# A linear-attention kernel with a dense gated layer: second group's attention later, key rows copied by GpSimd, three f-tiles begun on two thirds of their tokens, last outputs on two queues

## The chip, the cores and the metric

The kernel runs on one core of one Trainium2 chip. Its engines are TensorE (PE, with its weight loads shown apart as PEld), VectorE (DVE), ScalarE (ACT), GpSimd (POOL) and SyncE (SP), whose queue issues most of the DMAs. The metric is the device time of one execution in microseconds (us).

## The reference

A linear attention with a decaying state runs over 4 batches, 8 heads, 768 steps and a head size of 48. Its result, as 3072 tokens of 384 values, goes through a dense layer of 2048 columns with the gate h·tanh(softplus(h)).

```python
for t in range(S):                      # per batch and head
    cur = (u * k[t]) v[t]^T
    y[t] = r[t] (state + cur)
    state = w * state + k[t] v[t]^T
x = y as (B * S, H * D)                 # 3072 x 384
h = x @ w_in                            # 384 x 2048
g = h * tanh(softplus(h))
out = g @ w_out                         # 2048 x 384
```

## The kernel before, in words

**Attention.** A step handles a chunk of 64 positions for two of the four batches, so 128 tokens; there are 24 steps, and even and odd steps work on different batches with buffer sets 0 and 1 (`G`, `Wt`, `KI`). Of each step: `load_step` and `load_v` fetch r, k and v; `scale` (L483, DVE) multiplies r and k by powers of the decay; `halves` (L467) copies halves of them to the buffers, by ACT or DVE in the first three steps and by DMA (L471) later; `diag` (L502 on ACT or L504 on DVE) scales keys by u; `keys` (L539) makes the key rows; `attend` lets PE make scores (`pa`, L554) and DVE mask them (L594, the second mask takes the diagonal); `outputs` lets PE make the result (`yt`, L607, L620) and the next state (`st`, L664). ACT evacuates both (L693, L695, L680), PE transposes (L751), and ACT and DVE write the tokens to `x` (L720, L723).

`KI` holds key rows and, in the rows `DROWS`, the decay by which the state is carried: a diagonal block `ident * w^64`, written once for each of the two sets by eight ACT rows (`state_decay`, L263). Those of set 0 are made at the start; those of set 1 by `second_decay`, spread between other rows.

**Dense layer.** Three steps make a group of 384 tokens; there are eight groups. For a group the 16 f-tiles of 128 columns are gone through: `up` (L802 for group 0, which uses float32 weights whole, L778 for the others, in three products of float32r parts) accumulates an f-tile in one of two PSUM buffers `hp`; ACT or DVE copies it to `hb` (L892); four f-tiles make a batch, on which ACT runs three activations with two table loads (L813, L816, L819) and DVE multiplies (L828); `down` (L847, L778) then accumulates three outputs `acc0` to `acc2`. After a group they are copied to `ob` (L859) and written out (L860). The weights come as 64-bit floats: `convert_low` (L340, ACT) and `convert` (L357 or L359, L361, L363, L366, L368) make float32 of them during group 0, and `split` (L383, L385) makes the two parts.

**Order.** Each engine's instructions stand in one fixed order, which a planner in the kernel (`Flow`) makes from estimated costs when the program is built: each piece of work is a thread that yields the events it needs and the engine time it takes, and where two engines could do a copy the planner chooses. In PE's spare time ahead of the first f-tile the planner puts `keep_warm` products on zeros (L283). `place` says after which f-tile of the group before a step's attention may begin: it spreads the three steps of a group over the fractions from `LO0` to `HI0` (group 1) or `LO1` to `HI1` (the others) of that group's 16 f-tiles.

```python
n0, n = BESIDE.get(g) or (LAST[g - 1] + 1 - NF, NF)
lo, hi = (LO0, HI0) if g == 1 else (LO1, HI1)
at = (2 * (s - starts[g]) + piece) / (2 * GROUPS[g])
return n0 + min(n - 1, int((lo + at * (hi - lo)) * n))
```

Of the kernel before, what the change touches and what calls it, by code (L numbers as in the profile page):

```python
# [10 lines left out]
F32 = mybir.dt.float32  # L11
# [5 lines left out]
AF = mybir.ActivationFunctionType  # L17
# [4 lines left out]
B, H, S, D = 4, 8, 768, 48  # L22
NP = H // 2
# [6 lines left out]


SOON = 3
LENT = 2

UDIAG = 6
# [6 lines left out]
KT = DM // 128  # L42
NF = DFF // 128
NT = B * S
# [3 lines left out]
WG = 2  # L48
# [6 lines left out]
DROWS = (slice(0, D), slice(64, 64 + D))  # L55
# [3 lines left out]
GROUPS = [3] * 8  # L59
# [7 lines left out]
RK_BUFS = 2  # L67
GS = 2
LAG_US = 24.9
LO0, HI0, LO1, HI1 = 0.05, 0.9, 0.05, 0.8  # L70
AHEAD, HOLD_W = 2, 8
LAT, LAT0 = 0.15, 0.13
WARM0, WARM_MIN, FILL = 32, 0.3, 0.6
# [9 lines left out]
UNITS = [(ph, g, f) for ph, (g, f0, f1) in enumerate(PHASES) for f in range(f0, f1)]  # L83

BATCH, AT = [], []
for ph, (g, f0, f1) in enumerate(PHASES):
    n = 1 << int(math.log2(COLS // (128 * GROUPS[g])))
# [95 lines left out]
def pe(us):  # L183
    return {"pe": us}
# [3 lines left out]
def rwkv_mish_kernel(ctx, tc, rkT, rkN, vN, wT, w_in, w_out, consts, rkF, vF, wF, uF, outT):  # L188
    nc = tc.nc
# [5 lines left out]
    ps = ctx.enter_context(tc.tile_pool(name="ps", bufs=1, space=PSUM))  # L195
# [11 lines left out]
    ident = cst[:, 128:256]  # L207
# [4 lines left out]
    early = const.tile([128, 1], F32, name="early")  # L212
# [5 lines left out]
    KI = [const.tile([128, 2, 2, NP, D], F32, name=f"KI{i}") for i in range(2)]  # L218
# [24 lines left out]
    w64 = pw[:, 6]  # L243
# [13 lines left out]
            mul = pw[:, m].unsqueeze(1).unsqueeze(3).broadcast_to([128, 2, NP, n])  # L257
            nc.vector.tensor_tensor(out=both(n, C - 2 * n, n), in0=both(0, C - n, n), in1=mul, op=ALU.mult)

    def state_decay(i, par, p):  # L260

        r = DROWS[par]
        nc.scalar.activation(  # L263
            KI[i][r, par, :, p, :], ident[r, r].unsqueeze(1).broadcast_to([D, 2, D]), AF.Copy, scale=w64[r, p : p + 1]
        )

    def token_table():
# [7 lines left out]
                )  # L275
        nc.scalar.copy(out=TKn, in_=t[:, : NP * D].rearrange("t (p d) -> t p d", d=D))

    idle = ps.tile([128, 512], F32, name="idle", tag="hp", bufs=2)

    def keep_warm(n):  # L280

# [5 lines left out]
    nc.vector.tensor_tensor(out=uw, in0=wu[:, 1], in1=wc, op=ALU.mult)  # L287
    for par in range(2):
        for p in range(NP):
            state_decay(0, par, p)  # L290
    token_table()

    flow = Flow(FREE)
    flow.events.update(READY)
    flow.fill = lambda us: keep_warm(int(us * FILL / 0.112))
    ok = const.tile([32, 1], I32, name="ok")

    def second_decay():
        for par in range(2):
            for p in range(NP):  # L300
                yield {"act": 0.3}
                state_decay(1, par, p)
        flow.set("decay")

    def check_range():

# [19 lines left out]
    raws, wholes, parts = {}, {}, {}  # L326
# [65 lines left out]
    xs = {}  # L392
# [237 lines left out]
    def outputs(s):  # L630
        q = s % 2
        last = s >= NS - NQ

        more = TURN <= s < NS - 1
        yield f"moved{s}"
        yield f"placed{s}"
        yield f"keys{s}"
        yield f"v{s}"
        if s == 1:
            yield "decay"  # L640
        if s:
            yield f"y{s - 1}"
            yield f"state{s - 1}"
            if GROUPS[0] <= s <= TURN:
                yield f"x{s - 1}"
        if more:
            yield f"scaled{s + 1}"
            yield f"masked{s}"
        yield from paced(s, 1)
        yield pe((1.0 if last else 1.8 if s >= TURN else 2.0) + (0.9 if more else 0))  # L650
        y = ps.tile([128, 512], F32, name="yt", tag="yt")
        st = ps.tile([128, 512], F32, name="st", tag="st")

        for p in range(NP):
            for a in range(2):
                for b in range(2):
                    tokens(q, y, p, a, b) if s < TURN else rows(q, y, p, b, a)
        if not last:
            for c in range(2):
                for p in range(NP):  # L660
                    for par in range(2):
                        k = slice(0, (128, 112)[par])
                        n = (c * NP + p) * D
                        nc.tensor.matmul(  # L664
                            st[DROWS[par], n : n + D],
                            lhsT=KI[q][k, par, c, p, :],
                            rhs=Wt[q][k, par, c, p, :],
                            start=True,
                            stop=True,
                        )  # L670
        if more:
            pas[s + 1] = scores(s + 1, loaded[s + 1][0][:, 1], "pa")
            flow.set(f"scores{s + 1}")
        flow.set(f"out{s}")
        flow.start((evacuate_y if s < TURN else direct)(s, y), rank(s) - L_FIN)
        if not last:
            for par in range(2):
                r = DROWS[par]
                engine = yield {**act(384), **dve(384)}
                (nc.scalar.copy if engine == "act" else nc.vector.tensor_copy)(  # L680
                    out=Wt[q][r, par].rearrange("d c p e -> d (c p e)"), in_=st[r, : 2 * NP * D]
                )
        flow.set(f"state{s}")
# [108 lines left out]
    def by_tile(o, t):  # L792
        return t[:, : o.n * o.T].rearrange("p (j t) -> p j t", j=o.n)

    def up(o, j):
        f, T = o.f + j, o.T
        hp = ps.tile([128, 512], F32, name="hp", tag="hp", bufs=2)
        w = (wholes if o.whole else parts)[0, f // WG]
        for k in range(KT):
            fs = slice((k * WG + f % WG) * 128, (k * WG + f % WG + 1) * 128)  # L800
            if o.whole:
                nc.tensor.matmul(hp[:, :T], lhsT=w[:, fs], rhs=o.x[:, 0, k, :T], start=k == 0, stop=k == KT - 1)  # L802
                continue
            three(
                hp[:, :T], w[:, 0, fs], w[:, 1, fs], o.x[:, 0, k, :T], o.x[:, 1, k, :T],
                k == 0, k == KT - 1,
            )
        return hp[:, :T]
# [45 lines left out]
    def put(engine, mt, T, cols):  # L854
        if cols.stop == NT and mt == KT - 1:
            ob = work.tile([128, COLS], F32, name="ob", tag="fa", bufs=1)
        else:
            ob = stage.tile([128, TM], F32, name="ob", tag="we", bufs=WE_BUFS)
        (nc.scalar.copy if engine == "act" else nc.vector.tensor_copy)(out=ob[:, :T], in_=accs[mt][:, :T])  # L859
        nc.scalar.dma_start(outT[mt * 128 : (mt + 1) * 128, cols], ob[:, :T])  # L860


    batches = {}
# [1 line left out]
    def up_tile(n):  # L865
        ph, g, f = UNITS[n]
        b, j = AT[n]
        T = GROUPS[g] * 128
        if f == 0:
            for s in range(starts[g], starts[g] + GROUPS[g]):  # L870
                yield f"x{s}"
        if j == 0 and 2 <= b < len(BATCH) - 1:
            yield f"gated{b - 2}"
        yield f"{'w' if g else 'v'}0,{f // WG}"
        if n >= 2:
            yield f"h{n - 2}"
        yield pe(unit_us(n))
        flow.fill = None
        if j == 0:
            batches[b] = new_batch(T, xs[g], f, len(BATCH[b]), not g, b == len(BATCH) - 1)  # L880
        o = batches[b]
        flow.start(evacuate(n, o, j, up(o, j)), n - L_EVAC)
        if n == BATCH[b][-1]:
            flow.start(gate(b, o, BATCH[b]), n - L_GATE)
        if n == LAST[g]:
            flow.set(f"ups{g}")
        if not g and f % WG == WG - 1:
            flow.set(f"used{W_ORDER.index((0, f // WG))}")
# [72 lines left out]
    def ffn():  # L961
        d = 0
        for n in range(len(UNITS) + 1):
            if n < len(UNITS):
                yield from up_tile(n)
                flow.set(f"u{n}")
            while d < len(UNITS) and AFTER[d] <= n:
                yield from down_tile(d)
                d += 1
# [3 lines left out]
            flow.start(thread(s), rank(s) + k / 1000 - (L_V if group[s] and thread is load_v else 0), 0.0)  # L973
    flow.start(check_range(), -100, 0.0)
    flow.start(load_weights(), -500, 0.0)
    flow.start(second_decay(), -1000.5, 0.0)
    for c in range(len(W_ORDER)):
        i, f = W_ORDER[c]
        n = FIRST[f * WG]
        flow.start(convert_low(c), (AFTER[n] - L_OUT if i else n - L_IN) + c / 1000 - AHEAD, 0.0)  # L980
        flow.start(convert(c), (AFTER[n] - L_OUT if i else n - L_IN) + c / 1000, 0.0)
        n += NF
        flow.start(split(c), (AFTER[n] - L_OUT if i else n - L_IN) + c / 1000, 0.0)
    flow.start(ffn(), 1000, 0.0)
    flow.run()
    assert not flow.parked, list(flow.parked)
# [152 lines left out]
```

## Time and profile before

| | |
|---|---|
| time, median of 3 runs | 531.26 us (529.8, 531.26, 535.85) |
| the profiled execution | 530.0 us, span of its trace 528.2 us |
| PE busy | 510.8 us (97% of the span) |
| PE weight loads busy | 470.1 us (89%) |
| ACT busy | 402.8 us (76%) |
| DVE busy | 323.3 us (61%) |
| POOL busy | 6.0 us (1%), 19 instructions |
| PE's mean granted clock | 0.994 |

The profile comes from one execution. Busy shares are means over the whole span, and this kernel has two stages with different loads: the first 50 us, with the attention of group 0 and the conversion of the weights, and the rest, where the dense layer runs. They have to be read apart. PE's busy time in the first stage contains the products on zeros.

### The profile page before, as it was taken

Reading aid. Unit: us, or ns where it says so; the run is one execution under the profiler, and the core shown is the slowest. Engines: PE = TensorE matmul, PEld = TensorE weight load, DVE = VectorE, ACT = ScalarE, POOL = GpSimd, SP = SyncE. Lnnn points to the kernel's source line nnn. Section 1 sums busy time; section 2 is a strip of 40 time slices with the busy share of each in tenths; the row PEclk is TensorE's granted clock in tenths of the full one; section 3 lists DMA queues with packets and bytes.
Section 4 is the critical chain, followed back from the end, with each engine's and each line's share of the span. In section 5 each row is a group of like instructions: output and inputs, shape, how many; then the busy total and the mean of one; then the engine's idle time right before and its main releaser. Section 6 shows DMA issues by size and latency. Waiting matters only on the chain.

```text
span 528.2 us, 11442 instructions
## 1 busy us (share of the span) xinstructions
PE 510.8 (97%) x4765; PEld 470.1 (89%) x4765; DVE 323.3 (61%) x489; ACT 402.8 (76%) x501; POOL 6.0 (1%) x19
## 2 busy tenths in 40 slices
PE   8887999999999999999999999999999999999994
PEld 6754666687999999999999999999999999999993
DVE  6998998765676575474664475474474473334341
ACT  6999957669798668667887768667687767777882
POOL 4000000000000000000000000000000000000000
PEclk9999899999999999999999999999999999999998
DMA  8998444113443244323443243323333250001001
GB/s 238 414 374 274 130 132 130 45 37 92 115 115 106 59 149 114 86 74 103 119 114 104 63 151 108 97 59 107 117 116 104 66 153 17 2 2 45 1 0 49
DMA packets 31051, 57.88 MB, mean 110 GB/s; under 512 B 6064, under 2 KB 19248, under 8 KB 30992
## 3 DMA queue, kind: packets, MB, share of 16 engines
q1 hardware_dynamic: 27392, 52.13, 33.9%
q10 hardware_dynamic: 3600, 4.95, 2.7%
q8 instruction: 39, 0.64, 0.5%
q14 instruction: 20, 0.16, 0.1%
HBM read 36.80 MB, written 4.72 MB: 79 GB/s over the span
## 4 chain that ended last, share of the span: by engine, by line
PE 80%; ACT 7%; DVE 4%; DMA 3%; SPq 2%; issue 2%; ACTq 0%; DVEq 0%
PE hp L778 30%; PE acc L778 27%; PE hp L802 6%; PE acc L847 5%; PE pa L554 5%; PE yt L620 3%; PE st L664 2%; SPq L743 1%; DMA rk<-in_rkT_dram 1%; ACT fa L816 1%; PE yt L607 1%; ACT wraw L340 1%; DMA rkn<-in_rkN_dram 1%; ACT L819 1%; DVE hb L828 1%
## 5 line engine op out<-in xcount | busy, mean ns | idle before, releaser
L778 PE MATMUL hp<-x,w 128*128 128x384 f32 x1008 | 197.0, 338 | 0.5 <-DMA x<-rkn 0.5
L778 PE MATMUL acc<-gh,w 128*128 128x384 f32 x672 | 187.8, 335 | 1.0 <-ACT gh L831 1.0
L778 PEld LDWEIGHTS hp<-x,w 128*128 128x128 f32 x1008 | 175.6, 188 | 3.8 <-DMA x<-rkn 0.8
L778 PEld LDWEIGHTS acc<-gh,w 128*128 128x128 f32 x672 | 122.8, 188 | 1.4 <-ACT gh L831 1.3
L778 PE MATMUL acc<-gl,w 128*128 128x384 f32 x336 | 112.3, 334 | 0.1
L892 ACT COPY hb<-hp 128x384 f32<-128x384 f32 x100 | 47.3, 474 | 59.6 <-PE hp L778 47.0
L828 DVE TENSOR_TENSOR hb<-hb,fa 128x768 f32<-128x768 f32 (+1 forms) x58 | 51.8, 927 | 39.9 <-ACT fa L819 39.9
L892 DVE COPY hb<-hp 128x384 f32<-128x384 f32 x28 | 15.6, 557 | 86.8 <-PE hp L778 84.1
L778 PEld LDWEIGHTS acc<-gl,w 128*128 128x128 f32 x336 | 63.1, 188 | 0.4 <-DVE gl L834 0.4
L831 ACT CAST gh<-hb 128x768 fp32r<-128x768 f32 (+1 forms) x58 | 47.2, 817 | 21.0 <-DVE hb L828 20.8
L834 DVE TENSOR_TENSOR gl<-hb,gh 128x768 fp32r<-128x768 f32 (+1 forms) x58 | 52.7, 928 | 7.6 <-ACT gh L831 5.8
L813 ACT ACTIVATE fa<-hb,bias_ln 128x1536 f32<-128x1536 f32 (+1 forms) x33 | 50.9, 1541 | 0.4
L816 ACT ACTIVATE fa<-fa 128x1536 f32<-128x1536 f32 (+1 forms) x33 | 47.8, 1449 | 2.0 <-ACT ob L859 1.7
L819 ACT ACTIVATE fa<-fa 128x1536 f32<-128x1536 f32 (+1 forms) x33 | 47.8, 1449 | 0.4
L819 ACT ACT_TABLE_LOAD x33 | 42.3, 1283 | 0.6
L813 ACT ACT_TABLE_LOAD x33 | 42.3, 1283 | 0.6
L483 DVE TENSOR_TENSOR rk<-rk,TRK 112x1024 f32<-112x1024 f32 x23 | 28.1, 1222 | 14.3 <-DMA rk<-in_rkT_dram 14.3
L847 PE MATMUL acc<-g,wraw 128*128 128x384 f32 x96 | 34.5, 496 | 0.0
L802 PE MATMUL hp<-x,wraw 128*128 128x384 f32 x96 | 33.2, 492 | 0.9 <-ACT x L720 0.9
L554 PE MATMUL pa<-rk 48*64 48x64 f32 x736 | 26.6, 222 | 4.7 <-DVE rk L483 3.5
L554 PEld LDWEIGHTS pa<-rk 48*64 48x64 f32 x736 | 23.4, 135 | 7.6 <-DVE rk L483 4.1
L802 PEld LDWEIGHTS hp<-x,wraw 128*128 128x128 f32 x96 | 18.4, 196 | 11.9 <-ACT x L720 1.1
(88 smaller groups left out, 452.5 us busy)
## 6 DMA issues: line engine op xcount, KB each, us to landing
rk<-in_rkT_dram SPq DMA_DIRECT2D x23, 448.0 KB, 4.2
rkn<-in_rkN_dram SPq DMA_DIRECT2D x18, 384.0 KB, 3.9
wraw<-in_w_in_dram SPq DMA_DIRECT2D x8, 768.0 KB, 12.1
wraw<-in_w_out_dram SPq DMA_DIRECT2D x8, 768.0 KB, 15.8
G<-rk SPq DMA_DIRECT2D x36, 128.0 KB, 2.3
out_dram<-ob ACTq DMA_DIRECT2D x24, 192.0 KB, 2.2
Wt<-in_vN_dram SPq DMA_DIRECT2D x46, 96.0 KB, 2.6
G<-rk SPq DMA_DIRECT2D x42, 96.0 KB, 2.4
```

The lines of the kernel that those rows point to most:

```text
L483: nc.vector.tensor_tensor(out=rk[:112], in0=rk[:112], in1=TRK[:112].unsqueeze(2).broadcast_to([112, 2, 2, NP, C]), op=ALU.mult)
L554: nc.tensor.matmul(pa[TROWS[par], n : n + C], lhsT=keys[r, c, p, :], rhs=rk[r, 0, c, p, :], start=True, stop=True)
L778: nc.tensor.matmul(out, lhsT=a, rhs=m, start=first and n == 0, stop=last and n == 2)
L802: nc.tensor.matmul(hp[:, :T], lhsT=w[:, fs], rhs=o.x[:, 0, k, :T], start=k == 0, stop=k == KT - 1)
L813: nc.scalar.activation(o.g, o.hb, AF.Sigmoid, bias=bias_ln2, scale=1.0)
L816: nc.scalar.activation(o.g, o.g, AF.Arctan)
L819: nc.scalar.activation(o.g, o.g, AF.Sin, scale=2.0)
L828: nc.vector.tensor_tensor(out=to[:, j], in0=o.hb[:, j], in1=o.g[:, j], op=ALU.mult)
L831: nc.scalar.copy(out=o.gh[:, j], in_=o.hb[:, j])
L834: nc.vector.tensor_tensor(out=o.gl[:, j], in0=o.hb[:, j], in1=o.gh[:, j].bitcast(F32), op=ALU.subtract)
L847: nc.tensor.matmul(accs[mt][:, :T], lhsT=w[:, ws], rhs=o.gh[:, j], start=first, stop=last)
L892: (nc.scalar.copy if engine == "act" else nc.vector.tensor_copy)(out=o.hb[:, j], in_=h)
```

## The change

Four edits.

1. `second_decay` and its eight ACT rows are gone. POOL copies the decay rows of set 0 to set 1 instead, right behind those of set 0. The two loops that do it stand in the code twice, so four copies run.
2. `LO0` goes from 0.05 to 0.25. The scores of steps 3, 4 and 5 may begin after f-tiles 4, 7 and 10 of group 0, where it was 0, 5 and 9.
3. For the f-tiles 0, 1 and 2 of group 0, a new thread `up_early` multiplies the 256 token columns of steps 0 and 1 as soon as these are there; `up` later adds the 128 columns of step 2. Tiles 0 and 1 use the two `hp` buffers, tile 2 uses the buffer of `acc0`. The buffer of the products on zeros moves to that of `acc1`.
4. In the last group the output that DVE copies is issued by SP's queue, where ACT's queue issued all three.

```diff
-LO0, HI0, LO1, HI1 = 0.05, 0.9, 0.05, 0.8
+LO0, HI0, LO1, HI1 = 0.25, 0.9, 0.05, 0.8
...
-    idle = ps.tile([128, 512], F32, name="idle", tag="hp", bufs=2)
+    idle = ps.tile([128, 512], F32, name="idle", tag="acc1")
...
     for par in range(2):
         for p in range(NP):
-            state_decay(0, par, p)
+            state_decay(par, p)
+    for par in range(2):
+        r = DROWS[par]
+        nc.gpsimd.tensor_copy(KI[1][r, par], KI[0][r, par])
+    for par in range(2):
+        r = DROWS[par]
+        nc.gpsimd.tensor_copy(KI[1][r, par], KI[0][r, par])
     token_table()
...
-    def second_decay():
-        for par in range(2):
-            for p in range(NP):
-                yield {"act": 0.3}
-                state_decay(1, par, p)
-        flow.set("decay")
...
+    def up_early(n):
+        g, f = UNITS[n][1:]
+        T = 128 * (GROUPS[g] - 1)
+        for s in range(GROUPS[g] - 1):
+            yield f"x{s}"
+        yield f"v0,{f // WG}"
+        yield pe(KT * 4 * T / 2400)
+        hps[n] = hp = ps.tile([128, 512], F32, name="hp", **(dict(tag="hp", bufs=2) if n < 2 else dict(tag="acc0")))
+        whole_up(hp, xs[g], f, slice(0, T))
+        flow.set(f"early{n}")
+
+    def whole_up(hp, x, f, at):
+        w = wholes[0, f // WG]
+        for k in range(KT):
+            fs = slice((k * WG + f % WG) * 128, (k * WG + f % WG + 1) * 128)
+            nc.tensor.matmul(hp[:, at], lhsT=w[:, fs], rhs=x[:, 0, k, at], start=k == 0, stop=k == KT - 1)
+
     def up(o, j):
         f, T = o.f + j, o.T
+        if o.whole and f in hps:
+            hp = hps.pop(f)
+            whole_up(hp, o.x, f, slice(T - 128, T))
+            return hp[:, :T]
...
-        nc.scalar.dma_start(outT[mt * 128 : (mt + 1) * 128, cols], ob[:, :T])
+        q = nc.sync if cols.stop == NT and engine == "dve" else nc.scalar
+        q.dma_start(outT[mt * 128 : (mt + 1) * 128, cols], ob[:, :T])
...
-        yield pe(unit_us(n))
+        if n < EARLY:
+            yield f"early{n}"
+        yield pe(unit_us(n) / (GROUPS[g] if n < EARLY else 1))
...
+    for n in range(EARLY):
+        flow.start(up_early(n), n, 0.0)
```

Since the planner lays out all engines anew, rows move that the diff does not name. (The line numbers after the change are higher by one or more.)

The first place is ACT's queue behind the constant table `TKn`. Before, `KI_85` (set 1) gets its decay there, row by row between the copies of r and of key rows:

```order
L276 COPY TKn<-yt 128x192
L263 ACTIVATE KI_85<-cst,pw 48x2x48
L467 COPY G_80<-rk 48x512
L263 ACTIVATE KI_85<-cst,pw 48x2x48
L467 COPY G_80<-rk 48x512
L263 ACTIVATE KI_85<-cst,pw 48x2x48
L467 COPY G_81<-rk 48x512
L263 ACTIVATE KI_85<-cst,pw 48x2x48
L467 COPY KI_84<-rkn 64x384
```

Now:

```order
L278 COPY TKn<-yt 128x192
L468 COPY G_80<-rk 48x512
L503 ACTIVATE gl<-rk,uw 112x2x64 x4
L468 COPY G_81<-rk 48x512
L503 ACTIVATE gl<-rk,uw 112x2x64 x4
L468 COPY G_81<-rk 48x512
L468 COPY KI_85<-rkn 64x384
L503 ACTIVATE gl<-gl,uw 112x2x64 x4
```

The decays are gone; the scaling of the keys of steps 0 and 1 by u (L503), which DVE did, has come to ACT, and one copy of r and two of key rows have gone to DVE.

The second place is PE's queue from step 2's outputs (`yt`, `st`) to the first down tile (`acc`). Before:

```order
L607 MATMUL yt<-Wt_82,G_80 64x48 x16
L664 MATMUL st<-Wt_82,KI_84 48x48 x16
...
L751 MATMUL t<-cst,G_80 128x128 x3
...
L802 MATMUL hp<-x,wraw 128x384 x3
L316 MATMUL ok<-inr,ones 32x4
L802 MATMUL hp<-x,wraw 128x384 x21
L554 MATMUL pa<-rk 64x64 x16
L554 MATMUL pa<-rk,gl 64x64 x16
L847 MATMUL acc_751<-g,wraw 128x384
```

Now:

```order
L608 MATMUL yt<-Wt_82,G_80 64x48 x16
L663 MATMUL st<-Wt_82,KI_84 48x48 x16
L811 MATMUL hp<-x,wraw 128x256 x6
L750 MATMUL t<-cst,G_80 128x128 x3
L811 MATMUL hp<-x,wraw 128x256 x3
L811 MATMUL hp<-x,wraw 128x128 x6
L317 MATMUL ok<-inr,ones 32x4
L811 MATMUL hp<-x,wraw 128x128 x3
L824 MATMUL hp<-x,wraw 128x384 x15
L869 MATMUL acc_669<-g,wraw 128x384
```

The 256-column parts of f-tiles 0 and 1 stand ahead of step 2's transposes, that of f-tile 2 behind them; the range check's product (`ok`) stands behind the rests of f-tiles 0 and 1; and step 3's scores (`pa`) no longer stand between the eighth f-tile and the first down tile. They now follow the second down tile and the tenth f-tile.

The third place is DVE's queue around step 2's `G`, whose last two copies release step 2's outputs on PE. Before:

```order
L594 COPY_PREDICATED gl<-cst,pa 128x512
L366 SCALAR_TENSOR_TENSOR we<-wraw,we 128x768
L594 COPY_PREDICATED gl<-cst,pa 128x512
L368 ISA wraw<-wraw,we 128x768x2
L467 COPY G_80<-gl 64x512
L361 TENSOR_SCALAR we<-we 128x768
L467 COPY G_80<-gl 64x512
```

Now:

```order
L595 COPY_PREDICATED gl<-cst,pa 128x512
L468 COPY Wt_82<-rkn 64x384
L468 COPY KI_84<-rkn 64x384
L595 COPY_PREDICATED gl<-cst,pa 128x512
L468 COPY KI_84<-rkn 64x384
L468 COPY G_80<-gl 64x512
L364 TENSOR_SCALAR we<-we 128x768
L468 COPY G_80<-gl 64x512
```

The two long conversion rows (L366, L368) have gone from between the masks and the copies.

More of the change, by code (lines that the diff above doesn't have):

```diff
@@ L32 @@
 SOON = 3
+EARLY = 3
 LENT = 2
@@ L258, in powers, with state_decay @@
             nc.vector.tensor_tensor(out=both(n, C - 2 * n, n), in0=both(0, C - n, n), in1=mul, op=ALU.mult)
-    def state_decay(i, par, p):
+    def state_decay(par, p):
         r = DROWS[par]
         nc.scalar.activation(
-            KI[i][r, par, :, p, :], ident[r, r].unsqueeze(1).broadcast_to([D, 2, D]), AF.Copy, scale=w64[r, p : p + 1]
+            KI[0][r, par, :, p, :], ident[r, r].unsqueeze(1).broadcast_to([D, 2, D]), AF.Copy, scale=w64[r, p : p + 1]
         )
@@ L638, in outputs @@
         yield f"v{s}"
-        if s == 1:
-            yield "decay"
         if s:
@@ L793, in by_tile @@
         return t[:, : o.n * o.T].rearrange("p (j t) -> p j t", j=o.n)
+    hps = {}
+    def up_early(n):
[13 more added lines that the diff above has]
+            nc.tensor.matmul(hp[:, at], lhsT=w[:, fs], rhs=x[:, 0, k, at], start=k == 0, stop=k == KT - 1)
     def up(o, j):
         f, T = o.f + j, o.T
+        if o.whole and f in hps:
+            hp = hps.pop(f)
+            whole_up(hp, o.x, f, slice(T - 128, T))
+            return hp[:, :T]
         hp = ps.tile([128, 512], F32, name="hp", tag="hp", bufs=2)
@@ L975, in rwkv_mish_kernel @@
     flow.start(load_weights(), -500, 0.0)
-    flow.start(second_decay(), -1000.5, 0.0)
     for c in range(len(W_ORDER)):
```

## The prediction

> **What bounds the kernel now.** I read the table of stretches first (busy us per engine, then PE's granted clock, the DMA share and GB/s), then the chain that ended last.
>
> ```profile
> core 0: us, PE busy (x) PEld busy (x) DVE busy (x) ACT busy (x) POOL busy (x), PEclk, DMA share, GB/s
> 10.00:50.00 40.00, 35.39 (x489) 25.81 (x484) 37.01 (x64) 37.17 (x64) 0.00 (x0) 1.00 1.02 370
> 57.00:157.00 100.00, 100.00 (x974) 78.33 (x974) 77.17 (x113) 77.82 (x98) 0.00 (x0) 1.00 0.37 100
> 157.00:200.00 43.00, 42.46 (x400) 41.18 (x399) 27.13 (x41) 32.42 (x40) 0.00 (x0) 1.00 0.39 110
> 200.00:300.00 100.00, 100.00 (x970) 98.14 (x969) 57.10 (x83) 74.18 (x88) 0.00 (x0) 1.00 0.36 98
> ```
>
> From 57 on PE never stops, but for 43.00 - 42.46 = 0.54 us, while DVE and ACT have a quarter of their time free or more. There PE is the bound, and what it gains before comes off the end. From 10 to 50 it is the other way round: ACT is idle for 2.83 us of 40 and DVE for 2.99, and part of PE's busy time is filler that keeps its clock up. So the question is when ACT and DVE let PE begin, and whether PE then runs on. The chain shows the place where they hold it (start, duration, what; the seven f-tiles after the first, then a wait, then scores and the first down tile):
>
> ```profile
> 36.30 13.76 PE hp L802 x42
> 50.07 0.02 issue
> 50.09 0.56 DVE hb L892
> 50.65 0.86 DVE wraw L368
> 51.52 0.87 DVE we L366
> 52.39 1.14 DVE rk L483
> 53.53 0.04 issue
> 53.57 3.03 PE pa L554 x64
> 56.60 2.75 PE acc L847 x6
> ```
>
> ```profile
> 50.89 1.48 ACT L819 ACTIVATE fa<-fa 128x1536 f32<-128x1536 f32 x1
> ```
>
> One f-tile of six records takes 6 x 13.76/42 = 1.97; the eighth ends at 50.06. Batch 0's activation ends on ACT at 50.89 + 1.48 = 52.37. DVE does four other rows first, PE resumes at 53.57 with step 3's scores and has the first down tile at 56.60. The ends to move are ACT's 52.37 and PE's 53.57. When the first f-tile starts matters only through them.
>
> **The change part by part.** First ACT, from the constant table (near 9) to the end of batch 0's activation. The groups by shape give busy us in all, then mean ns of one:
>
> ```profile
> L340 ACT ACTIVATE wraw<-wraw 128x768 f32<-128x768 uint32 x16 | 14.5, 928 | 0.1
> L357 ACT ACTIVATE we<-wraw 128x768 f32<-128x768 f32 x10 | 9.3, 930 | 1.1 <-DVE wraw L368 1.1
> ...
> L892 ACT COPY hb<-hp 128x384 f32<-128x384 f32 x11 | 5.2, 477 | 11.4 <-PE hp L802 11.4
> L263 ACT ACTIVATE KI<-cst,pw 48x96 f32<-48x96 f32 x16 | 5.2, 364 | 2.7 <-DVE iw L246 2.6
> ...
> L502 ACT ACTIVATE gl<-rk,uw 112x128 f32<-112x128 f32 x8 | 2.5, 394 | 0.0
> L693 ACT COPY G<-yt 128x288 f32<-128x288 f32 x6 | 2.4, 397 | 1.0 <-PE yt L607 1.0
> L467 ACT COPY KI<-rkn 64x384 f32<-64x384 f32 x4 | 2.0, 511 | 0.1
> L467 ACT COPY G<-gl 64x512 f32<-64x512 f32 x3 | 1.9, 618 | 0.3 <-DVE gl L594 0.3
> ```
>
> Out of that stretch of ACT's queue go the eight second decays (8 x 0.364 = 2.91), three low-word conversions (L340, 14 to 11: 2.78), two of L357 (5 to 3: 1.86) and three key copies (4 to 1: 1.53), 9.08 in 16 rows. In come two scalings of step 0 and 1, which DVE did before (8 rows of L502: 3.15), two more f-tile copies (4 to 6: 0.95) and one more G copy (at most 0.62), 4.72 in 11 rows. That is 4.36 less. Neighbours overlap (8 x 0.394 = 3.15, busy 2.5: 0.08 each), which takes 5 x 0.08 = 0.4 off. ACT's waits gain little: down its new queue I find 0.4 for step 2's scaling, 0.65 for step 0's second mask, 1.5 while the first three f-tiles come off PE and 0.4 of small ones, 2.95 against 2.83. So **ACT ends 3.9 earlier**; the conversions are deferred, not gone. I put the end at 48.5.
>
> Then PE. The rows of it around step 1's and 2's outputs:
>
> ```profile
> 26.79 0.55 PE L751 MATMUL t<-cst,G 128*128 128x128 f32 x3 [0.67 <-ACT G L695]
> 27.17 1.36 PE L283 MATMUL idle<-zeros 128*128 128x256 bf16 x11
> 28.46 1.17 PE L607 MATMUL yt<-Wt,G 128*64 128x48 f32 x32
> 29.46 1.02 PE L664 MATMUL st<-Wt,KI 128*48 128x48 f32 x32
> ```
>
> Step 2's state products end at 30.48. ACT is 1.3 earlier when it releases these transposes, and DVE's two copies of step 2's G now stand ahead of weight rows, so the filler in between goes: I put that end at 28.1 (at the old 30.48 PE would be through at 48.1, which still hides). From there PE has f-tiles 0 and 1 on 256 columns (two thirds of 2 x 1.97: 2.6), step 2's transposes (0.55), f-tile 2 on 256 columns (1.3), and the 128-column rests. These are 18 records of a shape that the trace lacks: by columns 0.11 each, by a full record 0.33. I take 0.18 from the transposes, which have the same load and columns (0.55/3): 3.3, with ends at 2.0 and 5.9. Five whole tiles follow (9.85). The sum is 28.1 + 17.6 = 45.7, 4.4 before the old 50.06.
>
> The first product of batch 0 follows ACT's end.
>
> ```profile
> L828 DVE TENSOR_TENSOR g<-hb,fa 128x768 f32<-128x768 f32 x8 | 7.3, 953 | 0.6 <-ACT fa L819 0.6
> ```
>
> Half of batch 0 takes 0.95, so the first down tile starts at 48.5 + 1.0 = 49.5, and step 3's scores no longer stand ahead of it. PE is idle from 45.7 to 49.5: a wait of **3.8 in place of 3.5**, now for ACT. PE resumes at 49.5 instead of 53.57: **-4.1**. Of the 4.4 of the early tiles most turns into that wait. With the rests at 5.9 PE ends at 48.3 and ACT's batch moves about 1 later; at 2.0 nothing changes.
>
> DVE must be there too. Its row for the range check (L318) now waits for PE behind the rests of two tiles, some 2.3, with the conversion for f-tiles 6 and 7 queued behind it; 12 us of rows later it reaches the product at 47.7. That covers the wait by 0.8; more comes off the 4.1.
>
> POOL's four key-row copies have no row. The nearest is its memset of that size:
>
> ```profile
> L226 POOL MEMSET Wt<- 48x384 f32 x4 | 1.5, 418 | 0.1
> ```
>
> The copies start when the first decays are done, near 7.7; two mask memsets (about 0.5 each) queue behind them, and the first mask is due at 13.9. Up to 1.3 each they cost nothing; I take 0.45, so 0. At 2.0 each the start slips 2.8.
>
> From the resumption to f-tile 16 PE has the same instructions, and before it did not wait there.
>
> ```profile
> 101.72 1.58 PE hp L778 x9
> ```
>
> What can be late are the outputs of steps 3 to 5, which need G by DMA after DVE's mask:
>
> ```profile
> G<-gl SPq DMA_DIRECT2D x6, 128.0 KB, 2.3
> ```
>
> Two such issues in a row cost about 3.5. With the durations above the three outputs come up 1 to 1.5 after their G. I take 0.5 off for what such a walk misses. Beyond, PE's 0.54 is a wait for x, whose chain leads back to a PE tile:
>
> ```profile
> 125.18 1.58 PE hp L778 x9
> 126.79 0.56 DVE hb L892
> ```
>
> So it moves along with PE: 0.
>
> The tail. ACT's queue issues the second output, which waits for DVE's copy, ahead of the third copy:
>
> ```profile
> 521.41 0.94 ACTq L860 DMA_DIRECT2D out_dram<-ob  x2
> 521.42 0.56 DVE L859 COPY ob<-acc 128x384 f32<-128x384 f32 x1 [2.35 <-PE acc L778]
> 521.57 0.34 PE L778 MATMUL acc<-gh,w 128*128 128x384 f32 x1
> 522.39 0.48 ACT L859 COPY ob<-acc 128x384 f32<-128x384 f32 x1 [1.01 <-DVE ob L859]
> ```
>
> With that issue on SP's queue, which has nothing else left, the third copy follows PE's end at 521.95: **-0.4**. The sum is -4.1 + 0.5 - 0.4 = **-4.0**, from the profiled execution's 530.0 (span 528.2) to 526.0. That execution lies low among the four known (529.8, 530.0, 531.26 and 535.85, middle 530.6), so I forecast 530.6 - 4.0 = **526.6**.
>
> **The rivals.** *Clock kept (0.2).* After its wait PE ran at a lower clock:
>
> ```profile
> 54.00:58.00 4.00, 4.00 (x61) 0.57 0.40 101
> ```
>
> It lost 4 x 0.43 = 1.7 of work, and I let it lose that again. If the new wait, shorter by my error or else placed, leaves the clock up, 1.7 more is saved: 524.9. The Trainium skill (TensorE: Matmul & The Clock Gate, Part 1) has the clock halve after an idle window of about 3.4 us that runs freely, so that equal waits can end either way. The trace agrees in length, 3.5.
>
> *POOL and DVE hold each other up (0.12).* If each POOL copy (0.42 to 0.51) stops DVE for its length between 7.7 and 12.7, step 0's masks come up to 2.0 later, and ACT and PE with them: 528.6. The trace is silent, since POOL only writes in it. The Trainium skill (SBUF — State Buffer, SBUF: two separate sides) says that a VectorE instruction with two SBUF inputs and a GpSimd one that reads SBUF exclude each other for the whole instruction. It speaks against this change.
>
> *The gain is given back (0.17).* The deferred conversions (2.78 + 1.86) come due between batch 0's and batch 1's activations. If PE waits there for batch 1, only the tail is left: 530.2. Against it: batch 1's product would be ready near 65, PE asks for it near 73.
>
> *Slower: the second group's tokens are late (0.08).* Its attention starts four f-tiles later and must still end before f-tile 16. If DVE's masks of steps 4 and 5 fall 3 behind my walk, the outputs of both and f-tile 16 wait about 2.2 each: 526.6 + 6.6 = 533.2. It decides when step 4's second mask ends after 77.
>
> **How the numbers follow.** The forecast has 0.43, with 524.5 to 529 as its own range. 522 to 531 leaves out the last rival and a little of each side. 1% is about what a measurement of this kernel can tell from no change; 1% below 531.26 is 525.95, which takes the fast third of the forecast (0.16) and most of the kept clock (0.18): faster 0.35, within 1% 0.59, slower 0.06.
>
> **What would show it.** Right: the first down tile near 49.5 with PE idle for 3 to 4 before it; f-tile 16 near 98 instead of 101.7; the third output copy within 0.1 of PE's end. Wrong: DVE rows stretched between 8 and 13, a new PE wait between 75 and 100, or a down tile not before 52.

## The result, and the profile after

The changed kernel takes 525.36 us (median of 6 runs, 524.44 to 527.7) against 531.67 us for the kernel before beside it (6 runs, 528.9 to 535.85). The ratio is 0.9892 with a 95% interval of 0.9865 to 0.9919, so it is 1.1% faster. The forecast was 526.6. The profiled execution took 524.44; its span of 522.7 is 5.5 less than that of before.

The table of stretches after the change (busy us of each engine, then PE's granted clock, the DMA share and GB/s):

```profile
10.00:50.00 40.00, 32.91 (x470) 25.92 (x466) 36.45 (x63) 36.73 (x62) 1.97 (x5) 0.98 1.01 370
57.00:157.00 100.00, 100.00 (x1044) 80.72 (x1043) 79.35 (x115) 80.18 (x107) 0.00 (x0) 1.00 0.37 102
157.00:200.00 43.00, 42.55 (x402) 41.52 (x401) 25.09 (x38) 33.31 (x39) 0.00 (x0) 1.00 0.38 107
200.00:300.00 100.00, 100.00 (x969) 98.14 (x969) 55.44 (x82) 75.28 (x88) 0.00 (x0) 1.00 0.36 101
```

From 57 on nothing is different in kind: up to 500 PE never stops but for 0.45 us near 160. What changed lies ahead of that. The chain of waits (start, duration, what):

```profile
35.85 9.70 PE hp L824 x30
45.55 3.39 issue
48.94 3.79 PE acc L869 x6
52.73 1.94 PE hp L824 x6
...
97.32 1.56 PE hp L777 x9
```

The rows of ACT and DVE that belong to its gap, from the timeline (in brackets the idle time ahead and what ended it), and PE's clock behind it, from the table of stretches for PE alone (stretch, length, busy us, clock, DMA share, GB/s):

```profile
46.36 1.49 ACT L841 ACTIVATE fa<-fa 128x1536 f32<-128x1536 f32 x1
47.88 1.83 DVE L850 TENSOR_TENSOR g<-hb,fa 128x768 f32<-128x768 f32 x2 [0.41 <-ACT fa L841]
```

```profile
49.00:53.00 4.00, 4.00 (x8) 0.60 0.22 66
```

Batch 0's activation ends at 47.85 instead of 52.37. DVE waits 0.41 for it, its first product follows, and the first down tile starts at 48.94. PE had gone on at 53.57 before: **4.63 earlier**. PE is idle for 3.4 us from 45.55, as long as before (3.5), and then runs four us at a clock of 0.60, which costs 1.6. F-tile 16 starts at 97.32 instead of 101.72, and PE's last product ends at 517.18 instead of 521.91: 4.73 earlier. The last rows:

```profile
516.84 0.34 PE L777 MATMUL acc<-gh,w 128*128 128x384 f32 x1
517.22 0.48 ACT L881 COPY ob<-acc 128x384 f32<-128x384 f32 x1 [0.56 <-PE acc L777]
517.28 0.35 SPq L884 DMA_DIRECT2D out_dram<-ob  x1
```

The third output copy now starts 0.04 behind PE's end, where it started 0.48 behind it.

### The profile page after: what moved, and what is told of

It is laid out like the page before. It is cut to its first block, busy times and chain, and to the rows that moved or that the text cites. A ratio compares the mean times of both kernels' runs of the same rounds, so it can differ in the third digit from the quotient of the medians.

```text
span 522.7 us, 11439 instructions
## 1 busy us (share of the span) xinstructions
PE 506.4 (97%) x4757; PEld 468.7 (90%) x4757; DVE 321.4 (62%) x486; ACT 402.3 (77%) x505; POOL 10.1 (2%) x23
## 4 chain that ended last, share of the span: by engine, by line
PE 84%; ACT 6%; DVE 3%; DMA 2%; issue 2%; SPq 2%; ACTq 0%
PE hp L777 30%; PE acc L777 28%; PE acc L869 6%; PE pa L555 5%; PE hp L824 5%; PE yt L621 3%; PE st L663 3%; PE yt L608 1%; SPq L742 1%; PE hp L811 1%; ACT L841 1%; ACT fa L841 1%; ACT fa L838 1%; DMA rk<-in_rkT_dram 1%; DVE rk L484 1%
## 5 line engine op out<-in xcount | busy, mean ns | idle before, releaser
L918 ACT COPY hb<-hp 128x384 f32<-128x384 f32 x104 | 49.2, 474 | 55.5 <-PE hp L777 47.2
L918 DVE COPY hb<-hp 128x384 f32<-128x384 f32 x24 | 13.4, 556 | 77.6 <-PE hp L777 77.4
L869 PE MATMUL acc<-g,wraw 128*128 128x384 f32 x96 | 35.6, 509 | 3.4 <-issue 3.4
L869 PEld LDWEIGHTS acc<-g,wraw 128*128 128x128 f32 x96 | 19.0, 204 | 14.0 <-issue 5.2
L824 PE MATMUL hp<-x,wraw 128*128 128x384 f32 x78 | 27.0, 490 | 0.0
```

The costliest lines, as they stand in the source:

```text
L869: nc.tensor.matmul(accs[mt][:, :T], lhsT=w[:, ws], rhs=o.gh[:, j], start=first, stop=last)
```

## The experiments

Two theories. Mine: the end of ACT's batch 0 sets when PE goes on, and from there PE is the bound and carries every microsecond to the end. The first rival: the f-tiles begun early carry the gain by themselves. The second: a gain at the resumption is given back before f-tile 16. Ratios are to the kernel before, run beside each.

**1. The wait filled, the clock kept.**

```diff
         yield pe(unit_us(n))
+        if not ph and f == f0:
+            keep_warm(24)
         down(batches[b], j, f == f0, f == f1 - 1)
```

> The changed kernel, with 24 products on zeros (128x256) put into PE's queue between the eighth f-tile and the first down tile, where PE waited 3.40 us for ACT and DVE. They wait for nothing and last about 24 x 0.12 = 2.9 us, so the wait itself stays and the first down tile still starts near 48.9. If PE's idle time is what lowers the granted clock (0.50 from 49 to 52), the first down tile takes about 2.0 instead of 3.79, everything behind it moves 1.7 earlier, and the span is near 521.0. If the clock falls for another reason, the tile still takes near 3.8 and the span stays at 522.7.

Measured: 523.18 us, ratio 0.9848 (0.9823 to 0.9873), span 521.0. PE's timeline, then its clock:

```profile
49.08 2.18 PE L869 MATMUL acc<-g,wraw 128*128 128x384 f32 x6 [0.80 <-PE idle L285]
```

```profile
49.00:53.00 4.00, 3.92 (x12) 1.00 0.51 101
```

The down tile starts where it did and takes 2.18 instead of 3.79. The 1.6 reach the end: span -1.7. PE's idle time is what lowers its clock there, and all that PE gains at this point is carried. One profile alone would not show the first part, since run 8 kept its clock behind an equal wait without a filler; but five of this run's six times (522.78 to 523.39) lie below all six of the changed kernel (524.44 to 527.7). From the resumption to PE's end I count 517.18 - 48.94 - 1.61 = 466.6 in the changed kernel, 515.65 - 49.08 = 466.6 here, and 521.91 - 53.57 - 1.7 = 466.6 before.

**2. F-tile 8 ahead of the first down tile.** `ffn` goes through f-tile 8 before down tile 0, and the batch buffer of f-tiles 8 to 11 is taken only when their copies are made.

```diff
-            while d < len(UNITS) and AFTER[d] <= n:
+            while d < len(UNITS) and AFTER[d] + (d == 0) <= n:
```

> The changed kernel, with the ninth f-tile (number 8) ahead of the first down tile instead of behind it. Its weights are ready at 43.1, its PSUM buffer is free at 45.1; its copy to the batch buffer still waits for batch 0's product. If ACT's end of batch 0 (47.85) and DVE's product (0.98) set when PE can go on, and all later work is PE's, the f-tile fills 2.0 of the 3.4 us wait, the rest of 1.4 is too short to lower the clock, the first down tile starts near 48.9 at full clock, and the lead of 2.0 + 1.7 = 3.7 is carried to the end: span near 519.0. If the work behind is held by ACT or DVE (the rival that the gain is given back), a new wait of PE appears between 55 and 100 and the span stays above 521.

Measured: 528.36 us, ratio 0.9947 (0.9926 to 0.9969), span 524.9, slower than the changed kernel. The first half was right and the second wrong. PE's timeline:

```profile
49.17 4.12 PE L871 MATMUL acc<-g,wraw 128*128 128x384 f32 x12 [1.50 <-issue]
...
94.99 0.55 PE L750 MATMUL t<-cst,G 128*128 128x128 f32 x3 [0.55 <-ACT G L694]
96.74 0.44 PE L777 MATMUL hp<-x,w 128*128 128x384 f32 x1 [1.20 <-ACT x L719]
...
160.44 0.76 PE L777 MATMUL hp<-x,w 128*128 128x384 f32 x3 [1.37 <-DMA x<-rkn]
```

The wait shrank to 1.50, two down tiles ran at full clock, and PE was through with f-tile 9 3.4 us ahead of the changed kernel. Then it waited 0.55 at step 3's transposes (69.66) and 1.75 ahead of f-tile 16 (first for ACT's copy of step 5's result, then for ACT's copy of its tokens). By the down tile behind f-tile 16 the lead was gone (98.86 against 98.72; the rows next to a wait take longer too), and near 160 PE waited 2.3 more. The second rival is real, though not in the changed kernel.

**3 and 4. Without the third edit; without the first.** Run 3 has no early f-tiles (`EARLY = 0`). Run 4 writes set 1's decay by eight ACT rows again:

```diff
-    for par in range(2):
-        r = DROWS[par]
-        nc.gpsimd.tensor_copy(KI[1][r, par], KI[0][r, par])
...
+    flow.start(second_decay(), -1000.5, 0.0)
```

> The changed kernel without its third edit: no f-tile is begun on 256 columns. By my theory (ACT's queue up to batch 0's third activation sets when PE goes on) this moves little: ACT's queue has one conversion more (0.93), I walk it to an end near 49.2, the first down tile near 50.2, with the eighth f-tile ending near 47.5 and a wait of some 2.7. That is 1.3 later than the changed kernel, span near 524.0 if the clock falls all the same, and 522.3 if the shorter wait leaves it up. By the rival, in which the early f-tiles carry the gain, the 4.4 us that the eighth f-tile had gained go, and the span is near 527.

> The changed kernel without its first edit: set 1's decay rows are again eight ACT rows (0.364 each), and POOL copies nothing. By my theory ACT's queue up to batch 0's end is longer by what the order shows: 8 decays 2.9, two conversions 1.9, three key copies 1.5, less eight scalings 3.2 and one G copy 0.6, so 2.5. ACT ends near 50.3, the first down tile starts near 51.4, and the span is near 525.2, although the early f-tiles are all there and PE waits some 5 us. By the rival (the early f-tiles carry the gain) the span is near 523.5, as the eighth f-tile ends only 0.8 later. If POOL's copies cost DVE something that mattered, it comes out below 525.

Measured: run 3 532.86 us, ratio 1.0009 (0.9984 to 1.0034), span 532.1; run 4 531.56 us, ratio 0.9997 (0.9973 to 1.0021), span 527.3. Neither differs from the kernel before. I had expected spans of 524.0 and 525.2. In both, ACT's end is followed by the resumption as the theory says: ACT ends at 52.01 and 49.03, the first down tile starts at 53.05 and 50.12. But much is lost elsewhere. Run 4, PE's timeline around f-tile 16, then its clock:

```profile
97.46 0.55 PE L753 MATMUL t<-cst,G 128*128 128x128 f32 x3 [0.55 <-ACT G L697]
99.21 0.44 PE L780 MATMUL hp<-x,w 128*128 128x384 f32 x1 [1.20 <-ACT x L722]
```

```profile
98.00:102.00 4.00, 2.64 (x9) 0.74 0.43 116
102.00:106.00 4.00, 4.00 (x40) 0.83 0.10 25
```

These are the waits of run 2, and here the clock falls behind them (0.26 x 4 + 0.17 x 4, up to 1.7 of work). The changed kernel has no such wait, because its planner put an f-tile between step 5's outputs and its transposes, and a down tile between these and f-tile 16 (its timeline of PE; L663 belongs to the outputs):

```profile
91.05 1.14 PE L608 MATMUL yt<-Wt,G 128*64 128x48 f32 x32
92.01 0.89 PE L663 MATMUL st<-Wt,KI 128*48 128x48 f32 x32
92.83 2.21 PE L824 MATMUL hp<-x,wraw 128*128 128x384 f32 x6
94.88 0.49 PE L750 MATMUL t<-cst,G 128*128 128x128 f32 x3
95.21 2.11 PE L869 MATMUL acc<-g,wraw 128*128 128x384 f32 x6
```

In runs 2, 3 and 4 only one down tile stands there. Run 3 also lost time at the start, where its clock was at 0.54 to 0.61 for eight us, and ACT, which waited for PE there, came later with all that follows. This belongs to the profiled execution (533.9): three others of this kernel (529.32 to 530.09) had spans of 527.5 to 528.3. The clock of run 3:

```profile
16.00:20.00 4.00, 3.97 (x76) 0.54 1.02 418
20.00:24.00 4.00, 4.00 (x92) 0.61 1.02 413
```

The second edit changes no row here. With `LO0` at 0.05 in the changed kernel, the planner writes the same rows in the same order on all five engines, with the early f-tiles and without them. It adds nothing there; the scores of step 3 go behind the first down tile for other reasons (they do in runs 3 and 4 too, whose rows don't depend on `LO0` either). In the kernel before, 0.25 alone would move them.

**5, 6 and 7. The order ahead of f-tile 16.** Down tile 7 waits for step 5's outputs to be issued, and down tile 8 for its transposes, so that PE has a down tile, the transposes, an f-tile and a down tile there. Run 5 does that to run 4, run 6 to run 2, run 7 to run 3.

```diff
+HOLD = {7: 'out5', 8: 'turned5'}
...
         yield f"g{n}"
+        if n in HOLD:
+            yield HOLD[n]
```

> The run with ACT's decays again, and two down tiles of group 0 (numbers 7 and 8) held back: number 7 until step 5's outputs are issued, number 8 until step 5's transposes are, so that PE has work between these and f-tile 16. My theory: in that run the resumption (50.12, at full clock) cost nothing against the changed kernel; what made it 4.6 longer was PE's order ahead of f-tile 16 (waits of 0.55, 1.20 and 0.15 there) and the clock that these waits lowered (98 to 106, some 1.7). With cover at most the 0.55 is left: span 527.3 - 1.35 - 1.7, near 524.2. If the late ACT rows themselves cost the time, it stays near 527.

> The run with f-tile 8 ahead of the first down tile, with the same two down tiles held back. If its lead was given back ahead of f-tile 16 (0.55 and 1.20), 1.2 to 1.7 of it stays: span near 523.4 by that alone; if the later waits for x by DMA near 160 (1.37, 0.39, 0.53, against 0.45 in the changed kernel) shrink too, near 521.6. By the rival that ACT and DVE can't follow a PE that is 3.5 ahead, a new wait appears elsewhere before 200 and the span stays near 525.

> The run without the early f-tiles, with the same two down tiles held back. My theory: its waits of 0.55 and 1.20 ahead of f-tile 16 and the lower clock after them (102 to 110, some 1.7) go, so 532.1 - 1.2 to 3.0, that is 529 to 531, and what is left over the changed kernel's 522.7 is the later resumption (53.05 against 48.94, 4.1) and what the low clock between 16 and 22 costs. If the order ahead of f-tile 16 explains nothing, it stays at 532.

Measured: run 5 528.31 us, ratio 0.9943 (0.9918 to 0.9968), span 526.5; run 6 528.04 us, 0.9935 (0.9915 to 0.9954), span 525.7; run 7 529.95 us, 0.9975 (0.9952 to 0.9999), span 526.3. By the ratios run 5 is 2.9 us faster than run 4, clear of noise, and run 7 1.8 faster than run 3, with intervals that overlap, so the order does explain a part; run 6 is no better than run 2. In none of them is the place free of waits. The waits at the transposes and at f-tile 16 go, and the outputs of step 5, now asked for earlier, wait for G by DMA (PE's timeline of run 5, then of run 6):

```profile
91.65 0.32 PE L610 MATMUL yt<-Wt,G 128*64 128x48 f32 x4 [1.15 <-DMA G<-gl]
```

```profile
88.54 0.32 PE L609 MATMUL yt<-Wt,G 128*64 128x48 f32 x4 [2.26 <-DMA G<-gl]
```

Run 6, whose PE comes earliest, waits longest (2.26, against 1.13 to 1.15 in runs 5 and 7): the tokens of the second group are nearly late in all of these. This is the mechanism of the slower rival in the prediction, at another price. In run 6 the clock fell behind that wait too (0.57 from 90 to 94, 1.7 of work).

Run 5's span did not fall to 524.2 for two reasons. It waited 1.35 for G, where 0.55 had been expected to stay, and its clock did another thing behind the same wait as in run 4, which made its first down tile 1.4 longer (clock of runs 4 and 5 from 50 to 54; the waits ahead of it were 3.07 and 3.06). Two executions of run 5 at a mean clock of 0.999 had spans of 524.1 and 524.2.

```profile
50.00:54.00 4.00, 3.88 (x12) 1.00 0.14 38
```

```profile
50.00:54.00 4.00, 3.83 (x7) 0.60 0.10 33
```

**8. POOL copies once.** One of the two loops goes, so two copies run instead of four.

> The changed kernel with POOL copying the two blocks of decay rows once instead of twice (2 copies, not 4). If POOL's copies and DVE's rows of two SBUF inputs hold each other up (a copy took 0.50 alone and 1.55 beside them; DVE's two key-row products 0.61 each instead of 0.55, its copy of G 0.61 instead of 0.42), these rows return to their short times, DVE's first mask starts 0.3 to 0.6 before 13.99, and PE's scores of step 2 the same before 14.75. Down the line this is hidden: ACT's queue sets the resumption, which moves by at most 0.3. Span 522.4 to 522.8. If the copies had cost the path something, it is 1 or more below 522.7.

Measured: 524.61 us, ratio 0.9876 (0.9841 to 0.9912), span 522.8: no different from the changed kernel. First the timeline of POOL and DVE in the changed kernel, then in this run:

```profile
6.15 0.50 POOL L295 COPY KI<-KI 48x384 f32<-48x384 f32 x1 [0.46 <-ACT KI L265]
7.33 1.55 POOL L295 COPY KI<-KI 48x384 f32<-48x384 f32 x1 [0.68 <-ACT KI L265]
7.29 2.67 DVE L484 TENSOR_TENSOR rk<-rk,TRK 112x1024 f32<-112x1024 f32 x2
9.99 0.61 DVE L468 COPY G<-rk 48x512 f32<-48x512 f32 x1
```

```profile
7.33 1.55 POOL L295 COPY KI<-KI 48x384 f32<-48x384 f32 x1 [0.68 <-ACT KI L265]
7.29 1.23 DVE L481 TENSOR_TENSOR rk<-rk,TRK 112x1024 f32<-112x1024 f32 x1
10.65 0.42 DVE L465 COPY G<-rk 48x512 f32<-48x512 f32 x1
```

A copy takes 0.50 alone and 1.55 when it begins beside DVE's scaling: it ends 0.36 behind that row (8.88 against 8.52), as if it had waited for it. In return DVE's copy of G takes 0.61 beside POOL's copies and 0.42 without them. The Trainium skill (SBUF — State Buffer, SBUF: two separate sides) has a VectorE instruction of two SBUF inputs and a GpSimd one that reads SBUF shut each other out. The rows of the scaling, which has two, agree; the copy of G has one, so its 0.19 is another matter. On DVE POOL's rows cost some 0.7: these 0.19, 0.31 in the pair of scalings, which took 2.36 in run 5 without any copy, and 0.19 in the pair of key-row products (1.22 against 1.03). The time shows nothing of that, but it could not: the intervals of run 8 and the changed kernel overlap, and they are 3.8 and 2.9 us wide. Nor did DVE's first mask come earlier, as expected (14.22 for 13.99), since the second scaling of this execution had to wait for r and k:

```profile
9.39 1.23 DVE L481 TENSOR_TENSOR rk<-rk,TRK 112x1024 f32<-112x1024 f32 x1 [0.87 <-DMA rk<-in_rkT_dram]
```

This run kept its clock behind a wait of 3.41 (its first down tile took 2.18), and lost it ahead of 20 instead (0.64 from 16 to 20). Behind the wait it was 1.25 ahead of the changed kernel (f-tile 8 at 51.32 against 52.57), and at PE's end 0.05: its waits at the x of the third group near 160 were 0.20, 0.42 and 0.52, where the changed kernel has one of 0.45. Ahead of that f-tile the lead was still 1.06 (the last product there starts at 157.37 against 158.43), behind it 0.06 (160.97 against 161.03). So 1.0 is given back at this place, 0.7 of it as idle time. The last part of x came when it did in the changed kernel, although PE was ahead.

**9 to 12. Both clock losses filled.** The early wait (1.7 us ahead of step 2's scores near 13) also lowers the clock in some executions, so these four have both fillers: run 9 all edits, run 10 no third edit, run 11 no first edit (both with the held down tiles), run 12 no fourth edit.

```diff
-    flow.fill = lambda us: keep_warm(int(us * FILL / 0.112))
+    flow.fill = lambda us: keep_warm(int(us * (0.85 if us > 2.3 else FILL) / 0.112))
```

> The changed kernel with the 24 products on zeros ahead of the first down tile and 6 more of them (20 for 14) ahead of step 2's scores, where PE waited 1.7 us near 13 and the clock fell behind that wait in some profiles (0.59 to 0.64 from 16 to 20) and not in others. If a lower clock comes only from these two waits, every execution now keeps it: span 521.0 as in the run with the first filler alone, and the times lie closer together, median at or a little below 523.2. If the filler gets in the way of step 2's scores, they start after 14.75 and the span is 521.5 or more.

> Without the early f-tiles, two down tiles held back, and both fillers (20 products ahead of the first down tile). With the clock up everywhere, the difference to the run with all edits and both fillers is what the third edit is worth: the first down tile near 51.3 instead of 49.0 (ACT then waits for whole f-tiles before its batch: 0.67 and 1.82 in the run before), and the outputs of step 5 wait 1.3 for G by DMA. Span near 524.5, 3.5 over it. If the early f-tiles only turn into a longer wait of PE, as I had reckoned, the first down tile stands within 0.5 of 49.0 and the span within 2 of 521.0.

> With the decays on ACT again, two down tiles held back, and both fillers. With the clock up everywhere, the difference to the run with all edits and both fillers is what the first edit is worth: the first down tile near 50.1 instead of 49.0 (1.1), and 1.35 that the outputs of step 5 wait for G by DMA. Span near 523.5. If the first edit is worth what its eight rows take (2.9), the first down tile is near 52.

> All edits but the fourth (the last group's three outputs are issued by ACT's queue), and both fillers. Nothing moves but the tail: the third output copy waits behind the issue of the second, and starts 0.4 to 0.5 behind PE's end instead of 0.04. Span 521.4 to 521.5. If the end is set by the landing of the other outputs, it stays at 521.0.

Measured: run 9 525.64 us, ratio 0.9900 (0.9874 to 0.9926), span 523.6; run 10 527.81 us, 0.9955 (0.9939 to 0.9971), span 525.5; run 11 527.0 us, 0.9928 (0.9904 to 0.9952), span 525.8; run 12 525.73 us, 0.9912 (0.9887 to 0.9937), span 522.4. Run 9 is slower than run 1, from which it differs in six products on zeros. They did keep the clock up from 16 to 20 (1.00), but PE then stood still where nothing that the profile shows held it (PE's timeline of run 9):

```profile
29.99 0.24 PE L663 MATMUL st<-Wt,KI 112*48 112x48 f32 x1 [1.64 <-issue]
30.16 4.55 PE L811 MATMUL hp<-x,wraw 128*128 128x256 f32 x12
```

and the early f-tiles behind that ran at a lower clock (0.59 from 30 to 32, 0.56 from 32 to 34), 4.55 where 12 records took 2.87 in run 12. So fillers are not free: these six cost 2.5 by the medians.

Runs 10 and 12 both had the stall of 1.64 and a full clock to the end, so they can be compared: first down tile at 51.56 without the third edit and 50.44 with it, 1.1. The early f-tiles gain in one place and lose in another. From the start of step 2's transposes to ACT's end it takes 19.6 without them (runs 3, 7 and 10) and 16.3 with them, 3.3 less, since ACT's copies wait less for PE (0.8 for 2.5 in run 7) and two conversions fewer stand there. But two of them stand ahead of these transposes and, with the stall, delay them by 2.2 here (33.10 against 30.94). The 1.1 is the least that they are worth at the resumption: the stall took 1.5 from them in run 12 (the changed kernel transposes at 31.60). Against the changed kernel's own 48.94 it is 2.6, and 3.3 by run 7 (52.23, with a lower clock at the start). At PE's end run 10 is 3.2 behind run 12 (520.11 against 516.89): 1.1 from the resumption, 1.3 from its wait for G, and 0.7 in PE's rows that I did not take apart. Run 11 does not give the first edit's price: in this execution step 1's r and k landed late, and DVE's second scaling waited 1.53 for them. Run 5 does, since it had no such wait and a full clock before: 50.17 against 48.94, so **1.2 at the resumption**.

Run 12's third copy starts at 517.47, 0.58 behind PE's end, so the fourth edit takes 0.54 off ACT's last copy. In the time it can't be seen: from PE's end to the end of the span the executions vary from 5.2 to 6.3, whichever queue is used (run 12 5.51, the changed kernel 5.52).

## Why the prediction was right, point by point

- **ACT's queue, -3.9 to 48.5.** Right in the sum, low by 0.65 (47.85): every profile but that of before has the first down tile 1.04 to 1.10 behind ACT's end. But it is not ACT's rows alone that set this end. From the start of step 2's transposes on PE to ACT's end it took 20.4 before, and 16.25 to 16.31 in the changed kernel and in runs 1, 2, 6, 8, 9 and 12, whenever these transposes started (31.41 to 34.55). So 4.1 of the 4.5 come behind them, from the conversions that are deferred and from shorter waits for PE. ACT released the transposes 2.1 earlier (29.79 for 31.93, 1.3 in the prediction), but PE had two early f-tiles and its stall ahead of them and took them only 0.4 earlier, and ACT then waited 0.87 for PE. The prediction's remark that a later start of PE "still hides" is wrong: run 12's transposes came 1.50 later than the changed kernel's, and so did ACT's end (49.35). The rows of before, after (two) and run 12:

```profile
31.99 0.55 PE L751 MATMUL t<-cst,G 128*128 128x128 f32 x3 [0.85 <-ACT G L695]
```

```profile
31.60 0.49 PE L750 MATMUL t<-cst,G 128*128 128x128 f32 x3
32.12 0.48 ACT L719 COPY x<-t 128x384 f32<-128x384 f32 x1 [0.87 <-PE t L750]
```

```profile
33.10 0.49 PE L750 MATMUL t<-cst,G 128*128 128x128 f32 x3
```

  Some of it may be luck of the two executions: DVE's second scaling waited 0.46 for the DMA of r and k before (the row below) and not after, and its first mask began 0.55 earlier. How much of that reached ACT's end is not shown. In run 1 step 2's scores came 0.39 later than in the changed kernel and its transposes only 0.13, because PE's stall in between ended at nearly the same time.

```profile
9.27 1.23 DVE L483 TENSOR_TENSOR rk<-rk,TRK 112x1024 f32<-112x1024 f32 x1 [0.46 <-DMA rk<-in_rkT_dram]
```

- **The eighth f-tile, 45.7.** It ended at 45.55, by errors that cancel (PE's timeline):

```profile
29.87 1.89 PE L811 MATMUL hp<-x,wraw 128*128 128x256 f32 x8 [1.04 <-issue]
31.60 0.49 PE L750 MATMUL t<-cst,G 128*128 128x128 f32 x3
31.93 2.87 PE L811 MATMUL hp<-x,wraw 128*128 128x256 f32 x18
34.88 0.97 PE L811 MATMUL hp<-x,wraw 128*128 128x128 f32 x6
```

  The stall of 1.04 inside f-tile 1 I had not foreseen. The 18 records of 128 columns took (2.87 - 1.3 + 0.97)/18 = 0.14 each instead of 0.18, so 2.5 instead of 3.3, and step 2's state products ended at 27.8 for the 28.1 of the sum.
- **Most of the early tiles' 4.4 turns into the wait.** The wait was 3.4 (3.8 forecast). But they gave ACT more than I had reckoned, 1.1 to 3.3 at the resumption by runs 7, 10 and 12: ACT's copies of whole f-tiles waited 0.67 and 1.82 for PE in run 7, those of begun ones 0.23 and 0.58.
- **Resumption -4.1.** Measured -4.63. At this place the two edits nearly add up: 3.4 is left without the first (run 5, 50.17) and 1.3 without the third (run 7, 52.23). In the time they don't: without either, the kernel was no faster than before (runs 3 and 4), because of what came behind.
- **The range check's wait, 2.3 with 0.8 of cover.** Measured 2.42, and DVE still waited 0.41 for ACT.

```profile
34.99 0.15 DVE L319 TENSOR_REDUCE inr<-ok 32x1 f32<-32x4 f32 x1 [2.42 <-PE ok L317]
```

- **POOL's copies, 0.45 and nothing.** The first took 0.50; the rest were stretched as the rival said, and DVE's rows between 8 and 13 with them, which stood among the signs of being wrong; but the 0.7 on DVE is a third of the rival's 2.0. That the copies cost nothing in the end is not shown: run 8 only says that it is less than its interval can tell.
- **Carry to f-tile 16, 0.5 taken off.** Measured 4.40 of 4.63 there, and all of it at PE's end. This step was less safe than I had made it. Of the variants, every one with another order ahead of f-tile 16 lost 1.2 to 2.4 us there, some with a lower clock behind it. The two rivals of that kind had 0.17 and 0.08. Beyond f-tile 16 the wait for x near 160 moved along with PE (160.43 for 165.13), as forecast, but in run 8 it did not: there PE came 1.06 earlier and the last x did not.
- **Clock.** The loss recurred (1.6 for 1.7), as forecast. That it could as well have been kept is shown by runs 4 and 8.
- **Tail -0.4.** The copy moved by 0.44, and whether the time moved is not shown.

Of the 5.5 between the two spans 4.73 are at PE's end. The other 0.8 lie in what follows PE's end, which varies by as much from execution to execution.

## What to carry to other kernels

Read a gain at the place where the bound engine goes on again, and then look at the order of the next handover for what that engine has to do while it waits; a lead is worth only what that cover holds. Gains at one place need not add up in the time: here two edits nearly add up at the resumption (3.4 and 1.3 of 4.6), but each without the other was worth nothing in the end and both some 6 us, and a third changed no row beside them. When a queue gets shorter, ask which of its waits takes the gain back: here ACT was 2.1 earlier ahead of its wait for PE, and 0.4 behind it. A wait of the bound PE costs its length and, in some executions, as much as 1.7 us of lower clock; filling the long one with 24 products gave 523.18 us, the fastest version of all (0.9848 against 0.9892, with intervals that still overlap), while six more in another place cost 2.5.

## What the runs showed of the hardware

- The same wait ends with a full clock or with 0.6 of it: 3.40 (0.60) in the changed kernel and 3.41 (1.00) in run 8; 3.06 (0.60) in run 5 and 3.07 (1.00) in run 4; near 13, 1.71 (1.00 from 16 to 20) in the changed kernel and 1.71 (0.59) in run 2. Each fall costs 1.6 to 1.7. The Trainium skill (TensorE: Matmul & The Clock Gate, Part 1) names an idle window of about 3.4 us that runs freely, by which equal waits may end either way. The trace agrees in that, but not in the length: a wait of 1.71, with products on zeros before it, was enough in run 2.
- PE's stall near 29 ended at 29.87 in the changed kernel, 30.00 in run 1, 29.99 in runs 9 and 10, 29.69 in run 6 and 30.22 in run 12, and was 0.76 to 1.64 long. Runs 2 and 8, which have the same order there but came to these rows only at about 30, have no such stall. So it ends at a time, not after a length; what sets the time stays open.
